# Transposes of fp32 in 64-row tiles, two shared PSUM banks for them and for the rows of x, masks by bank, and constants spread over GpSimd's blocks

## The chip, the cores and the metric

The kernel runs on one core of one Trainium2 chip. The metric is the device time of one execution in microseconds, median of several runs. The engines are named as in the profile: PE is TensorE (PEld its weight loads), DVE VectorE, ACT ScalarE, POOL GpSimd, SP SyncE.

## What is computed

```python
# _attn_ref: q, k, v are [8, 8, 576, 64] (batch, heads, sequence, head_dim)
scores = scale * np.matmul(q, k.transpose(0, 1, 3, 2))
gamma = 1.0 - 2.0 ** (-5.0 - np.arange(H, dtype=np.float32))
Dmat = np.where(rel >= 0, gamma[:, None, None] ** rel[None, :, :], 0.0)
ret = scores * Dmat[None, :, :, :]
attn_out = np.matmul(ret, v)
# reference
x = attn_out.transpose(0, 2, 1, 3).reshape(B * S, H * D)      # [4608, 512]
# _moe_ref: w_gate [512, 8], w1 [8, 512, 1024], w2 [8, 1024, 512]
logits = x @ w_gate
expert_idx = np.argmax(logits, axis=1)
gate_w = probs[np.arange(N), expert_idx]                      # softmax of the logits
for e in range(E):
    mask = expert_idx == e
    out[mask] = gate_w[mask, None] * (np.maximum(x[mask] @ w1[e], 0.0) @ w2[e])
```

## The kernel before

Stage 1 is the attention (a retention with decay), up to about 180 us; stage 2 is the mixture of experts, up to the end. The order of the instructions on each engine is the order in which the program is written (a manual schedule); waits come from the buffers that a tile pool hands out and from the data.

The decay is split into a factor on q and one on k: POOL multiplies them in (`scale_q` L261 writes qq, `scale_k` L271 writes kk). Each batch has 576 positions, in five blocks (b, c): c=0 to 3 have 128 positions, c=4 has the last 64. Within a block the scores are masked, and what earlier blocks contribute comes through a running state (64x64 per head). The loop of L753 goes over the 40 blocks i and issues per block:

- `scale_q` and `scale_k(i+3)` on POOL, and the loads of k and v for block i+6 (q for the batch after the next) on SP; some blocks also load an expert's weights (POOL's queue, L249).
- T: `stage_TK(i+2)` and, for c>0, `stage_TQ` of the next batch. Each makes four fp32 transposes of 128x128 on PE (L63) into one PSUM bank (tiles psk and psq), and ACT copies the bank to SBUF (kT L293, qT L283).
- for c=1 `stage_L2`, the transposed router logits of the batch before.
- R: `stage_R(i-2)`, the bf16 rows of x: four transposes of xb into psr, copied by ACT (xr L420) and stored by SP to x_rows, from which stage 2 gathers.
- S: `stage_S(i+1)` adds k^T v to the state in the bank pss; ACT copies it (se L310). There is none when block i+1 has c=4. The tile se has two buffers, so in blocks c=1 and c=2 its copy waits until IN of the same block has read the older one.
- AV: `stage_AV(i)`, masked scores times v, into the two banks of psx; with c=4 this is part of the next step.
- for c=0 `stage_L1`, the router logits of the batch before, from xT and xTr (psl).
- IN: `stage_IN(i)`, the state times q, added in psx; then ACT copies psx twice, as xT (fp32, L373) and xb (bf16, L376). With c=4 ACT copies one half (xo), DVE adds the other to it (xTr L398), and ACT casts that (xb L401).
- SC: `stage_SC(i+1)`, the scores of the next block, into the two banks of pssc; DVE multiplies all 128x1024 by the mask in one operation (L328).
- from block (4,1) on, steps of the routing for the first half of the tokens, mostly on DVE (`route_first`).

PSUM has eight banks. Before, pssc has two, psx two, pss one, and a pool psw has three, which psk, psq, psr, the logits and the routing, and the first tiles of stage 2 take in turn. The constants of the router (`make_gate`, at i=3) and of the routing (`make_routing`, at i=5) are made on POOL, each in one run ahead of that block's scale_q.

After the loop come `stage_R(38)`, the transposes of the first gathered tokens (pt), `stage_L1(7)` and the first expert's `mm1` with `stage_L2(7)` and `stage_R(39)` between its parts. Stage 2 opens its own PSUM pools after that `mm1`.

## Time and profile before

| what | value |
|---|---|
| median of 3 runs | 350.86 us (349.3 to 351.81) |
| the profiled execution, its own time | 345.89 us |
| its span, first to last instruction | 344.2 us |
| PE busy | 321.0 us (93%) |
| ACT, POOL, DVE busy | 179.8, 200.6, 127.6 us |
| DMA queues | 65.25 MB, mean 190 GB/s |
| mean granted clock of TensorE | 0.985 of full speed |

A busy PE is not a PE at its peak: matmuls are pipelined, and their ends are modelled, so distances between starts say more than durations. In a timeline neighbouring instructions of one kind stand as one row with their count; in brackets is the idle time of the engine before it and what ended that. An fp32 matmul of L60 has two records, an fp32 transpose of L63 one. Blocks (b, c) can be told apart by their PE rows: c=0 has no psq, c=1 has psl from lt, c=3 has no pss, and c=4 has psx from kT.

### The profile page before, as it was taken

The numbers are of one execution on the slowest core, as the hardware profiler recorded it, in microseconds if no ns is written. First come the engines' busy times: TensorE is split into PE (matmuls) and PEld (weight loads), VectorE is DVE, ScalarE is ACT, GpSimd is POOL, SyncE is SP. The second block draws the span as 40 slices with busy tenths as digits, with TensorE's granted clock in tenths as the row PEclk, the third lists the DMA queues.
The fourth block names the chain that finished last, engine by engine and source line by source line (L and its number), as shares of the span: only waits on it lengthen the run. The fifth ranks groups of instructions, "written<-read, shape, count | busy, mean of one in ns | idle before, by whom it ended". The sixth has DMA issues, their size and how long they took to land. (4 is left out here: it accounts for less than half of the span.)

```text
span 344.2 us, 11063 instructions
## 1 busy us (share of the span) xinstructions
PE 321.0 (93%) x4662; PEld 238.2 (69%) x4662; DVE 127.6 (37%) x243; ACT 179.8 (52%) x365; POOL 200.6 (58%) x251
## 2 busy tenths in 40 slices
PE   6897999999999999899969989999999999999991
PEld 5676888888888888688857656555656566565650
DVE  5411422332336786369426852211212121211210
ACT  3554666674766666467555325455453535354440
POOL 3449454635356274884730247787788788887222
PEclk9998999999999999999999989999999999999997
DMA  8999989899987999999799114697999999999211
GB/s 206 236 209 232 232 205 223 204 229 222 212 199 187 239 216 227 230 259 228 146 203 184 60 61 153 125 191 186 201 165 214 213 195 222 214 218 223 83 53 77
DMA packets 112707, 65.25 MB, mean 190 GB/s; under 512 B 83470, under 2 KB 104974, under 8 KB 112656
## 3 DMA queue, kind: packets, MB, share of 16 engines
q0 software_dynamic: 18432, 31.47, 43.8%
q1 hardware_dynamic: 93696, 33.04, 41.4%
q8 instruction: 37, 0.61, 0.8%
q14 instruction: 14, 0.11, 0.1%
q10 hardware_dynamic: 528, 0.02, 0.1%
HBM read 67.13 MB, written 15.20 MB: 239 GB/s over the span
## 5 line engine op out<-in xcount | busy, mean ns | idle before, releaser
L271 POOL TENSOR_TENSOR kk<-kt,kg 128x512 f32<-128x512 f32 x39 | 41.5, 1064 | 69.7 <-PE pss L60 32.1
L715 ACT ACTIVATE ht<-pm 128x384 bf16<-128x384 f32 (+1 forms) x96 | 50.5, 526 | 55.6 <-PE pm L60 54.8
L60 PE MATMUL py<-w2b,ht 128*128 128x512 bf16 x320 | 76.1, 385 | 0.5 <-ACT ht L715 0.5
L60 PE MATMUL pm<-xt,w1b 128*128 128x256 bf16 (+1 forms) x512 | 72.5, 300 | 0.0
L858 DVE TENSOR_SCALAR ys<-py,gat 128x512 f32<-128x512 f32 x40 | 30.0, 750 | 108.6 <-PE py L60 96.8
L859 POOL DMA_INDIRECT out_dram<-ys,tids x40 | 40.9, 1022 | 47.5 <-DVE ys L858 31.0
L60 PEld LDWEIGHTS <-w1b 128*128 128x128 bf16 x512 | 50.0, 98 | 21.9 <-issue 0.6
L328 DVE TENSOR_TENSOR sc<-pssc,mask 128x1024 f32<-128x1024 f32 x32 | 39.1, 1223 | 48.3 <-PE pssc L60 45.9
L60 PEld LDWEIGHTS <-ht 128*128 128x128 bf16 x320 | 30.3, 99 | 31.6 <-issue 2.2
L658 POOL DMA_INDIRECT xg<-x_rows,tidg x40 | 41.0, 1024 | 15.3 <-issue 8.6
L60 PE MATMUL psx<-sc,vt 128*64 128x128 f32 (+1 forms) x640 | 38.6, 268 | 3.0 <-DVE sc L328 1.7
L60 PE MATMUL pssc<-qT,kT 64*64 64x128 f32 (+1 forms) x1024 | 35.0, 251 | 1.6 <-issue 1.5
L700 ACT COPY xt<-pt 128x512 bf16<-128x512 bf16 x40 | 22.7, 587 | 23.7 <-PE pt L63 23.7
L60 PEld LDWEIGHTS psx<-sc,vt 128*64 128x64 f32 (+1 forms) x640 | 30.9, 137 | 5.6 <-ACT kT L293 2.1
L60 PEld LDWEIGHTS pssc<-qT,kT 64*64 64x64 f32 x1024 | 28.7, 133 | 3.3 <-issue 2.7
L293 ACT COPY kT<-psk 128x512 f32<-128x512 f32 x40 | 23.6, 589 | 13.6 <-PE psk L63 13.3
L373 ACT COPY xT<-psx 128x512 f32<-128x512 f32 x32 | 18.9, 590 | 21.8 <-PE psl L60 11.6
L261 POOL TENSOR_TENSOR qq<-qt,qg 128x512 f32<-128x512 f32 x28 | 30.1, 1076 | 0.2
L63 PE MATMUL psk<-ident,kk 128*128 128x128 f32 x160 | 27.0, 293 | 0.8 <-POOL kk L271 0.8
L249 POOL DMA_DIRECT2D w2b<-in_moe_w_dram x32 | 24.0, 781 | 3.8 <-DMA w2b<-in_moe_w_dram 2.7
L310 ACT COPY se<-pss 128x256 f32<-128x256 f32 x32 | 12.4, 389 | 24.4 <-PE psx L60 23.3
L63 PE MATMUL psq<-ident,qq 128*128 128x128 f32 x128 | 19.5, 275 | 4.2 <-POOL qq L261 2.6
(126 smaller groups left out, 368.0 us busy)
## 6 DMA issues: line engine op xcount, KB each, us to landing
kt<-in_k_dram SPq DMA_DIRECT2D x32, 256.0 KB, 5.5
qt<-in_q_dram SPq DMA_DIRECT2D x16, 512.0 KB, 5.1
vt<-in_v_dram SPq DMA_DIRECT2D x32, 256.0 KB, 5.1
w1b<-in_moe_w_dram POOLq DMA_DIRECT2D x32, 256.0 KB, 6.1
w2b<-in_moe_w_dram POOLq DMA_DIRECT2D x32, 256.0 KB, 7.0
x_rows<-xr SPq DMA_DIRECT2D x32, 128.0 KB, 5.1
kt<-in_q_dram SPq DMA_DIRECT2D x8, 128.0 KB, 4.9
kt<-in_k_dram SPq DMA_DIRECT2D x8, 128.0 KB, 4.6
```

Source lines behind the costliest of these rows:

```text
L60: nc.tensor.matmul(out=out, lhsT=lhsT, rhs=rhs, start=start, stop=stop, skip_group_check=True)
L63: nc.tensor.transpose(out=out, in_=in_, identity=identity)
L249: after(nc.gpsimd.dma_start(out=wb[e][part // n][:, o:o + m, :], in_=w[e, o * P:(o + m) * P, :].rearrange("(c p) f -> p c f", p=P)), dep)
L261: eng.tensor_tensor(out=qq[:, :, :].rearrange("p s (h d) -> p h s d", d=DH), in0=qts[b][:, h0:h0 + 2, :, :], in1=qg[:, 0:NCH, h0:h0 + 2].r ...
L271: eng.tensor_tensor(out=kk[:, :, :], in0=kts.pop(i)[:, :, :], in1=kg[:, blocks[i][1], :].unsqueeze(2).to_broadcast([P, H, DH]), op=ALU.mult)
L293: mark["kT"] = nc.scalar.copy(out=kT[:, :, :].rearrange("p a t -> p (a t)"), in_=pst[:, :])
L328: mark["sc"] = nc.vector.tensor_tensor(out=sc[:, :, :, :].rearrange("p j a i -> p (j a) i"), in0=pssc[:, :, :].rearrange("p j (a i) -> p ( ...
L658: nc.gpsimd.indirect_dma_start(out=xg[:, :], out_offset=None, in_=x_rows[0:nr, :], in_offset=bass.IndirectOffsetOnAxis(ap=slots[ph][1][:, ...
L700: nc.scalar.copy(out=xts[(e, ph)][:, :, j * P:(j + 1) * P], in_=pt[:, :, :])
L715: nc.scalar.activation(out=ht[:, f0:f0 + per, :], in_=pm[:, :, :], func=AF.Relu)
L858: nc.vector.tensor_scalar(out=ys[:, :], in0=py[:, :], scalar1=gat[:, i:i + 1], scalar2=None, op0=ALU.mult)
L859: scatters.append(nc.gpsimd.indirect_dma_start(out=next(outs)[:, :], out_offset=bass.IndirectOffsetOnAxis(ap=tids[:, i:i + 1], axis=0), in ...
```

## The change

Five things are done, all in stage 1 and its end.

1. TK and TQ of a block become one `stage_T`. Each transpose of 128 rows becomes two of 64 rows (the upper and the lower half of the array's rows), which write to two different banks. These two banks are one tile pst2 with a single buffer; TK uses the left 256 columns of both banks, TQ the right. Both copies by ACT are issued after all transposes.
2. The rows of x (psr) take the same tag and so the same single buffer as pst2. R's transposes become twice as many, of 64 columns of xb each, and R stands behind AV. The pool psw keeps one bank.
3. The mask is two operations, one for each bank of pssc, and AV goes bank by bank.
4. `make_gate` comes at i=2, between scale_q and scale_k, with the memset of lg; `make_routing` is a generator, of which each block from i=7 on issues one piece.
5. In the first batch two of TQ's four parts go to psx and two to pst2. The PSUM pools of stage 1 are closed, and those of stage 2 opened, before `stage_R(38)`.

On ACT, in a block with c=2 (a full block with a state), this stood before (in brackets the engines and DMA queues whose semaphores an instruction waits for); kT and qT are T's copies, xr is R's, se the state's, xT and xb those of psx:

```order
L293 COPY kT<-psk 128x512 [waits PE_49]
L283 COPY qT<-psq 128x512 [waits PE_49]
L420 COPY xr<-psr 128x512 [waits DMAHW5_49,PE_49]
L310 COPY se<-pss 128x256 [waits PE_49,Activation_49]
L373 COPY xT<-psx 128x512
L376 CAST xb<-psx 128x512
```

and this stands after the change:

```order
L312 COPY kT<-pst_939 128x2x4x64 [waits PE_49]
L298 COPY qT<-pst_939 128x512
L342 COPY se<-pss 128x256 [waits PE_49,Activation_49]
L454 COPY xr<-psr 128x512 [waits DMAHW6_49]
L405 COPY xT<-psx 128x512
L408 CAST xb<-psx 128x512
```

xr has moved behind se, and qT has no wait of its own, since both copies wait for all of T.

On PE, in a block with c=4, this stood before (psk and psq are T, psr is R, pss is S, psx from sc is AV):

```order
L63 MATMUL psk<-ident,kk 128x128 [waits Activation_49,Pool_49]
L63 MATMUL psk<-ident,kk 128x128 x3
L63 MATMUL psq<-ident,qq 128x128 [waits Activation_49,Pool_49]
L63 MATMUL psq<-ident,qq 128x128 x3
L63 LDWEIGHTS xb
L63 MATMUL psr<-identb,xb 128x2x64 [waits Activation_49]
...
L60 MATMUL pss<-vt,kk 64x64 [waits DMAHW2_49]
L60 MATMUL pss<-vt,kk 64x64 x7
L60 MATMUL psx<-sc,vt 64x64 [waits DMAHW7_49,DVE_49,Activation_49]
```

and after the change:

```order
L63 MATMUL pst_660<-ident,kk 128x64 [waits Activation_49,Pool_49]
L63 MATMUL pst_660<-ident,kk 128x64 x7
L63 MATMUL pst_660<-ident,qq 128x64 [waits Pool_49]
L63 MATMUL pst_660<-ident,qq 128x64 x7
L60 MATMUL pss<-vt,kk 64x64 [waits DMAHW2_49]
L60 MATMUL pss<-vt,kk 64x64 x7
L63 LDWEIGHTS xb [waits PE_49]
L63 MATMUL psr<-identb,xb 64x2x64 [waits Activation_49]
...
L60 MATMUL psx<-sc,vt 64x64 [waits DMAHW7_49,DVE_49]
```

R's first transpose waited for nothing but its own input's copy and stood ahead of S; now it stands behind S, and its wait for ACT takes in the copies kT and qT, which read the same buffer.

On POOL, around the constants of the router (wgp), this stood before:

```order
L271 TENSOR_TENSOR kk<-kt,kg 128x512
L261 TENSOR_TENSOR qq<-qt,qg 128x2x4x64
L271 TENSOR_TENSOR kk<-kt,kg 128x512
L226 MEMSET wgp 128x256
L231 COPY wgp<-wgn 64x2x8 x8
L261 TENSOR_TENSOR qq<-qt,qg 128x2x4x64
L271 TENSOR_TENSOR kk<-kt,kg 128x512
```

and after the change:

```order
L269 TENSOR_TENSOR qq<-qt,qg 128x2x4x64
L279 TENSOR_TENSOR kk<-kt,kg 128x512
L269 TENSOR_TENSOR qq<-qt,qg 128x2x4x64
L233 MEMSET wgp 128x256
L238 COPY wgp<-wgn 64x2x8 x8
L244 MEMSET lg 128x320
L279 TENSOR_TENSOR kk<-kt,kg 128x512
L269 TENSOR_TENSOR qq<-qt,qg 128x2x4x64
```

The constants of the router, with lg, have moved ahead of one kk; those of the routing, which stood two pairs of qq and kk later in one run of fourteen with lg's memset, are in pieces of two from the eighth block on.

The diff, cut to its core:

```diff
     wk1 = p1.enter_context(tc.tile_pool(name="wk1", bufs=1))
     attc = p1.enter_context(tc.tile_pool(name="attc", bufs=1))
     rtmp = p1.enter_context(tc.tile_pool(name="rtmp", bufs=1))
-    ps1 = p1.enter_context(tc.tile_pool(name="ps1", bufs=1, space=PSUM))
-    psw = p1.enter_context(tc.tile_pool(name="psw", bufs=3, space=PSUM))
+    pp = ExitStack()
+    ps1 = pp.enter_context(tc.tile_pool(name="ps1", bufs=1, space=PSUM))
+    pst2 = pp.enter_context(tc.tile_pool(name="pst2", bufs=1, space=PSUM))
+    psw = pp.enter_context(tc.tile_pool(name="psw", bufs=1, space=PSUM))
+    pools = {"T": lambda *a: psw.tile(*a, tag="W", name="psw"),
+             "R": lambda *a: pst2.tile(*a, tag="t2", name="psr")}
 
 
...
@@ -272,26 +280,50 @@
                           in1=kg[:, blocks[i][1], :].unsqueeze(2).to_broadcast([P, H, DH]), op=ALU.mult)
         kks[i] = kk
 
-    def stage_TQ(b, p):
+    def pair_banks():
+        return pst2.tile([P, 2, 512], F32, tag="t2", name="pst2")
+
+    def put_TQ(ps, o, b, p):
 
         qq = qqs.pop((b, p))
-        pst = psw.tile([P, 512], F32, tag="W", name="psq")
         for s_ in range(NCH):
-            tr(pst[:, s_:512:NCH], qq[:, s_, :], ident[:, :])
+            for u in range(2):
+                r = slice(u * DH, (u + 1) * DH)
+                tr(ps[:, u, o + s_:o + 256:NCH], qq[r, s_, :], ident[r, r])
+
+    def get_TQ(ps, o, b, p):
+
         if b not in qTs:
             qTs[b] = wkp.tile([P, NP, 512], F32, tag="qT", name="qT")
-        nc.scalar.copy(out=qTs[b][:, p, :], in_=pst[:, :])
-
-    def stage_TK(i):
+        nc.scalar.copy(out=qTs[b][:, p, :].rearrange("p (u t) -> p u t", u=2), in_=ps[:, :, o:o + 256])
+
+    def put_TK(ps, o, i):
+
+        kk = kks[i]
+        for p in range(NP):
+            for u in range(2):
+                r = slice(u * DH, (u + 1) * DH)
+                tr(ps[:, u, o + p * DH:o + (p + 1) * DH],
+                   kk[r, 2 * p:2 * p + 2, :].rearrange("p h d -> p (h d)"), ident[r, r])
+
+    def get_TK(ps, o, i):
+
+        kT = wk3.tile([P, NP, P], F32, tag="kT")
+        mark["kT"] = nc.scalar.copy(out=kT[:, :, :].rearrange("p a (u t) -> p u a t", u=2),
+                                    in_=ps[:, :, o:o + 256].rearrange("p u (a t) -> p u a t", t=DH))
+        kTs[i] = kT
+
+    def stage_T(i, b, p):
+
         if i >= NB:
             return
-        kk = kks[i]
-        pst = psw.tile([P, 512], F32, tag="W", name="psk")
-        for p in range(NP):
-            tr(pst[:, p * P:(p + 1) * P], kk[:, 2 * p:2 * p + 2, :].rearrange("p h d -> p (h d)"), ident[:, :])
-        kT = wk3.tile([P, NP, P], F32, tag="kT")
-        mark["kT"] = nc.scalar.copy(out=kT[:, :, :].rearrange("p a t -> p (a t)"), in_=pst[:, :])
-        kTs[i] = kT
+        ps = pair_banks()
+        put_TK(ps, 0, i)
+        if p is not None:
+            put_TQ(ps, 256, b, p)
+        get_TK(ps, 0, i)
+        if p is not None:
+            get_TQ(ps, 256, b, p)
 
     def stage_S(i):
...
                         r = slice(j * DH, (j + 1) * DH)
                         mm(pssc[u * DH:(u + 1) * DH, j, p * P + u * DH:(p + 1) * P], kT[r, p, u * DH:(u + 1) * DH],
                            qT[r, p, c * P + u * DH:(c + 1) * P], True, True)
-            mark["sc"] = nc.vector.tensor_tensor(
-                out=sc[:, :, :, :].rearrange("p j a i -> p (j a) i"),
-                in0=pssc[:, :, :].rearrange("p j (a i) -> p (j a) i", i=P),
-                in1=mask[:, :].unsqueeze(1).to_broadcast([P, 2 * NP, P]), op=ALU.mult)
+            for j in range(2):
+                mark["sc"] = nc.vector.tensor_tensor(
+                    out=sc[:, j, :, :], in0=pssc[:, j, :].rearrange("p (a i) -> p a i", i=P),
+                    in1=mask[:, :].unsqueeze(1).to_broadcast([P, NP, P]), op=ALU.mult)
         else:
             qTs[(b, "r")] = kT
...
         if c < NCH:
             vt = vts.pop(i)
             sc = scs.pop(i)
-            for p in range(NP):
-                for j in range(2):
+            for j in range(2):
+                for p in range(NP):
                     o = (j ^ (p % 2)) * DH
                     mm(psx[o:o + DH, j, (p // 2) * P:(p // 2 + 1) * P], vt[:, 2 * p + j, :], sc[:, j, p, :],
...
@@ -405,7 +437,7 @@
         b, c = blocks[i]
         full = c < NCH
         n = NP if full else NP // 2
-        ps = psw.tile([P, n * P], BF16, tag="W", name="psr")
+        ps = pools["R"]([P, n * P], BF16)
         xb = xbs.pop(i)
         src = xb[:, :, :].rearrange("p w t -> p (w t)") if full else xb[:, :]
 
@@ -414,7 +446,9 @@
             w, a = k // (n // 2), k % (n // 2)
             o = ps[:, :].rearrange("p (h d) -> p h d", d=DH)
             o = o[:, 4 * a + w:4 * a + w + 3:2, :] if full else o[:, 2 * w:2 * w + 2, :]
-            tr(o, src[:, k * P:(k + 1) * P], (identb, identx)[w][:, :])
+            for u in range(2):
+                r = slice(u * DH, (u + 1) * DH)
+                tr(o[r], src[:, k * P + u * DH:k * P + (u + 1) * DH], (identb, identx)[w][:, :])
         xr = wk4.tile([P, n * P], BF16, tag="xr", name="xr")
         t0 = b * S + c * P
...
@@ -469,24 +502,29 @@
 
     def make_routing():
 
-        nc.gpsimd.memset(lg[:, :, :], 0.0)
         nc.gpsimd.memset(su1[:, :], -1.0)
         nc.gpsimd.affine_select(out=su1[:, :], in_=su1[:, :], pattern=[[-1, P]], base=0, channel_multiplier=1,
                                 compare_op=ALU.is_ge, fill=0.0)
+        yield
         nc.gpsimd.memset(onesb[:, :], 1.0)
         nc.gpsimd.iota(iota_r[:, :], pattern=[[1, P]], base=0, channel_multiplier=0,
                        allow_small_or_imprecise_dtypes=True)
+        yield
         nc.gpsimd.iota(rev[:, :], pattern=[[-1, E]], base=E, channel_multiplier=0,
                        allow_small_or_imprecise_dtypes=True)
         nc.gpsimd.memset(off[:, :], 0.0)
...
@@ -725,17 +763,22 @@
 
     keep_busy(12)
     scale_k(0, nc.vector)
-    stage_TK(0)
-    for p in range(NP):
+    stage_T(0, None, None)
+    for p in range(2):
         scale_q(0, p, nc.vector)
-        stage_TQ(0, p)
-        if p == 1:
-            keep_busy(8)
-            nc.vector.memset(pssc[:, :, :], 0.0)
+        put_TQ(psx, p * 256, 0, p)
+        get_TQ(psx, p * 256, 0, p)
+    keep_busy(8)
+    nc.vector.memset(pssc[:, :, :], 0.0)
+    ps = pair_banks()
+    for p in range(2, NP):
+        scale_q(0, p, nc.vector)
+        put_TQ(ps, (p - 2) * 256, 0, p)
+        get_TQ(ps, (p - 2) * 256, 0, p)
     nc.vector.memset(psx[:, :, 256:512], 0.0)
     scale_k(1)
     scale_k(2)
-    stage_TK(1)
+    stage_T(1, None, None)
     stage_SC(0)
     stage_S(0)
     load_k(5)
...
     for i, (b, c) in enumerate(blocks):
-        if i == 3:
-            make_gate()
-        if i == 5:
-            make_routing()
-
         if c > 0 and b + 1 < B:
             scale_q(b + 1, c - 1)
+        if i == 2:
+            make_gate()
         scale_k(i + 3)
+        if i > 6:
+            next(constants, None)
         fetch(early.get(i, 0))
         load_k(i + 6, mark.get("sc"))
-        stage_TK(i + 2)
-        if c > 0 and b + 1 < B:
-            stage_TQ(b + 1, c - 1)
+        stage_T(i + 2, b + 1, c - 1 if c > 0 and b + 1 < B else None)
         if c == 1 and b > 0:
             stage_L2(b - 1)
-        if i > 1:
-            stage_R(i - 2)
         if c in (1, 3) and b + 2 < B:
             load_q(b + 2, c // 2, mark.get("kT"))
         stage_S(i + 1)
         stage_AV(i)
+        if i > 1:
+            stage_R(i - 2)
         if c == 0 and b > 0:
             stage_L1(b - 1)
...
-    pools = {"T": lambda *a: psw.tile(*a, tag="W", name="pt"), "H": lambda *a: psw.tile(*a, tag="W", name="pm")}
+    pp.close()
+    pq = ExitStack()
+    psT = pq.enter_context(tc.tile_pool(name="psT", bufs=3, space=PSUM))
+    psH = pq.enter_context(tc.tile_pool(name="psH", bufs=3, space=PSUM))
+    psY = pq.enter_context(tc.tile_pool(name="psY", bufs=2, space=PSUM))
+    pools["T"] = pools["R"] = lambda *a: psT.tile(*a, tag="pt", name="pt")
+    pools["H"] = lambda *a: psH.tile(*a, tag="ph", name="pm")
```

## Rows read from the trace of the kernel before

**Rows 1.** Busy us (instructions) of the engines by stretch; granted clock, DMA share, GB/s.

```profile
30.00:33.40 3.40, 3.40 (x48) 2.95 (x45) 0.42 (x1) 1.58 (x4) 3.21 (x11) 0.50 1.19 241
...
40.00:60.00 20.00, 19.77 (x452) 17.36 (x448) 6.38 (x9) 13.10 (x28) 9.13 (x9) 1.00 0.91 218
```

**Rows 2.** Timeline of PE, block (2,2): start us, busy us, operation, count.

```profile
65.59 0.66 PE L63 MATMUL psk<-ident,kk 128*128 128x128 f32 x4
...
66.52 0.28 PE L63 MATMUL psr<-identb,xb 128*128 128x128 bf16 x2
...
66.83 0.69 PE L60 MATMUL pss<-vt,kk 128*64 128x64 f32 x16
67.35 1.05 PE L60 MATMUL psx<-sc,vt 128*64 128x128 f32 x16
68.33 0.67 PE L60 MATMUL psx<-qT,se 64*64 64x128 f32 x16
...
69.80 0.66 PE L63 MATMUL psk<-ident,kk 128*128 128x128 f32 x4
```

**Rows 3.** Timeline of ACT: block (1,4), then the end of block (2,2).

```profile
54.40 0.62 ACT L283 COPY qT<-psq 128x512 f32<-128x512 f32 x1
...
69.11 0.37 ACT L310 COPY se<-pss 128x256 f32<-128x256 f32 x1 [1.27 <-PE psx L60]
69.38 0.59 ACT L373 COPY xT<-psx 128x512 f32<-128x512 f32 x1
69.86 0.60 ACT L376 CAST xb<-psx 128x512 bf16<-128x512 f32 x1
```

**Rows 4.** Timeline of PE, block (1,3).

```profile
49.69 0.66 PE L63 MATMUL psk<-ident,kk 128*128 128x128 f32 x4
...
52.23 0.67 PE L60 MATMUL psx<-qT,se 64*64 64x128 f32 x16
```

**Rows 5.** Timeline of PE, block (1,4).

```profile
53.05 0.66 PE L63 MATMUL psk<-ident,kk 128*128 128x128 f32 x4
...
54.92 0.46 PE L60 MATMUL psx<-sc,vt 64*64 64x64 f32 x16
```

**Rows 6.** Timelines of PE and, last row, of DVE, block (2,0).

```profile
56.41 0.66 PE L63 MATMUL psk<-ident,kk 128*128 128x128 f32 x4
...
57.92 1.09 PE L60 MATMUL psx<-sc,vt 128*64 128x128 f32 x16
58.95 1.08 PE L60 MATMUL psl<-xT,wgp 128*32 128x128 f32 x32
...
56.56 1.22 DVE L328 TENSOR_TENSOR sc<-pssc,mask 128x1024 f32<-128x1024 f32 x1
```

**Rows 7.** Timeline of PE early in stage 1.

```profile
25.87 0.66 PE L63 MATMUL psk<-ident,kk 128*128 128x128 f32 x4
28.74 0.66 PE L63 MATMUL psq<-ident,qq 128*128 128x128 f32 x4 [2.21 <-POOL qq L261]
...
32.55 1.06 PE L63 MATMUL psk<-ident,kk 128*128 128x128 f32 x4
```

**Rows 8.** Timeline of POOL early in stage 1.

```profile
24.66 1.04 POOL L271 TENSOR_TENSOR kk<-kt,kg 128x512 f32<-128x512 f32 x1 [2.61 <-PE psx L60]
...
27.63 1.06 POOL L261 TENSOR_TENSOR qq<-qt,qg 128x512 f32<-128x512 f32 x1
```

**Rows 9.** Groups by line and form, weight loads: busy us, mean ns | idle before.

```profile
L63 PEld LDWEIGHTS psk<-ident,kk 128*128 128x128 f32 x160 | 17.4, 144 | 6.7 <-issue 3.1 <-POOL kk L271 2.3 <-POOL qq L261 0.5
...
L60 PEld LDWEIGHTS psl<-xT,wgp 128*32 128x32 f32 x256 | 6.5, 110 | 2.5 <-ACT xr L420 1.3 <-issue 1.2
```

**Rows 10.** Waits of PE, whole span: total us, times, longest us.

```profile
PE psx L60 <- DVE sc L328: 1.7, 7, 0.4
```

**Rows 11.** Timelines of DVE (first row) and PE at the end of stage 1.

```profile
179.24 0.42 DVE L398 TENSOR_TENSOR xTr<-psx,xo 128x256 f32<-128x256 f32 x1 [1.64 <-ACT xo L396]
...
180.64 1.08 PE L60 MATMUL psl<-xT,wgp 128*32 128x128 f32 x32 [1.10 <-ACT xr L420]
```

21 lines of the change are left out of this document (12 added, 9 removed).

## The prediction

> **What bounds the kernel now.** I read first the busy time by stretch, then TensorE's (PE's) order in time through one batch of stage 1, then what ScalarE (ACT), VectorE (DVE) and GpSimd (POOL) do beside it. In a steady stretch PE is busy 19.77 of 20 us, ACT 13.10, and the DMA engines carry a share of 0.91 [rows 1]: stage 1 goes by PE's order, with ACT and the loads not far behind. The change leaves the expert stage's arithmetic as it is, so every term below lies in stage 1 or at its end. Within a block I count from the start of its transposes (T). A block with c=2 lasts 4.21 us: T 0.93, rows of x (R) 0.31, state S 0.52, AV 0.98, then IN and scores 1.47 up to the next T [rows 2]. Blocks c=3 and c=4 each last 3.36 [rows 4 to 6].
>
> On ACT a copy of 128x512 follows its predecessor after 0.48 us when both are ready (0.27 after the half-sized se), and takes 0.59 to 0.62 [rows 3]. A mask of 1024 columns takes 1.22 us on DVE, and in c=0 AV starts 0.14 after its end (56.56 + 1.22 to 57.92) [rows 6]. I use 0.15 us for one engine's hand-over to another.
>
> **T itself.** TK and TQ are 8 instructions in 0.93 us, 0.116 each [rows 2]; after the change they are 16 that move 64 columns instead of 128. No row shows a 64-row tile with 128 columns. The nearest rows: 16 records of S move 64 columns in 0.52 us where 16 of AV move 128 in 0.98, so halving the columns halves a record; 16 records of IN use 64x64 tiles and take 0.48 for the same 128 columns where AV with 128x64 tiles takes 0.98, so two row halves run side by side [rows 2]. Both together would make T 16 x 0.116 / 4 = 0.47 us. Bounds: 0.47 if it is so, 0.93 if the loading of 128 columns sets the pace and T gains nothing. I take 0.47, because the row nearest in operation (IN's row halves) shows the full effect.
>
> On the load, the trace has 144 ns for one of 128 columns and 128 rows and 110 ns for one of 32 columns [rows 9]: a load overlaps others, and its time hardly follows its columns. The Trainium skill ("TensorE: Matmul & The Clock Gate", section "LDWEIGHTS (loading the stationary operand)") puts a load at columns/1.2 ns, whatever the number of rows: 107 ns for 128 columns, an estimate from that page, by which two 64-row tiles loaded side by side would take as long as one full tile and T would stay as it is. That is rival A's time below; the durations of these two rows do not follow that rule, though they do not settle the pace of a load either.
>
> **What the new order does with it, block by block.** T, TK's and TQ's output and R's output now share one buffer. R waits until both copies have read it, and qT's copy is behind kT's; and R's own copy xr now stands after se and ahead of xT and xb. All other work of a block keeps its length.
>
> c=1: T is 0.46 shorter, nothing new is late (the iteration before copies se without a wait): **-0.45**.
>
> c=2: in the iteration before, se waits for IN, so it starts 0.69 before T (69.11 against 69.80), and xT and xb come after it [rows 3]. With xr between, xb starts at -0.69 + 0.27 + 0.48 + 0.48 = 0.54, ends at 1.14, and AV, which overwrites what xb reads, starts at 1.29. T and S are done at 1.0, so PE waits 0.3. Then AV 0.98, R 0.31, IN and scores 1.47: 4.05 against 4.21, **-0.16**.
>
> c=3: no S. AV starts at 1.29 again; the first mask half, some 0.69 us long (an estimate: half of the 1.22 [rows 6] and 0.08 for a second start), is done before. AV ends at 2.27. kT is copied at 1.02, qT at 1.50 to 2.12, so R may start at 2.27 too. R 0.31, and from AV's end to the next T 0.82 as now (52.23 to 53.05) [rows 4, 5]: 3.40, **+0.04**.
>
> c=4: here R stands behind T and S on PE with no long AV before it. qT is copied 1.35 to 1.97 after T (54.40, 0.62 long) [rows 3, 5], set by xT, xb and kT ahead of it, not by PE; a faster T does not move it. R starts at 2.12, while T and S end at 1.1: 1.0 us of idle PE, and behind R stand AV, IN and the scores of the next block, all of PE's work. R 0.31 and 1.49 from AV to the next T (54.92 to 56.41) [rows 5, 6]: 3.92, **+0.56**.
>
> c=0: only TK. The mask's second half ends at 0.15 + 2 x 0.69 = 1.53, AV's second half (0.49) starts at 1.68, R ends at 2.48, where AV ends 2.54 after T's start now (56.41 to 58.95) [rows 6]: **-0.06**.
>
> Sum: -0.07 us a batch, over seven batches (the first goes by its loads) **-0.5 us**. If nothing waited it would be five TK and four TQ at 0.23 each, 2.1 us a batch: the copies give nearly all of it back.
>
> **The spread constants.** At 28.74 PE waited 2.21 us for a qq of POOL, and then ran at a granted clock of 0.50, the 1.2 GHz level, for 3.4 us [rows 1, 7]. That block lasted 6.68 us (25.87 to 32.55) against 3.36, 3.3 more, and the half clock reached 0.85 us into the next, 0.4 more: 3.7. The cause is on POOL: kk at 24.66, then the gate's memset and copies until qq at 27.63, 1.93 us [rows 8]. The change puts this work ahead of that kk, which waits 2.61 us for PE anyway [rows 8]. With one more memset (lg) it is somewhat over 2 us and fits. qq then runs at 25.70 and is done at 26.76; PE, done with TK at 26.1, waits 0.7 instead of 2.2, and I leave 0.2 for the two copies behind it. 3.7 - 0.9 = **-2.8 us**, between nothing (the wait only moves) and 3.7. The routing constants, in pieces of two, go into POOL's gaps: nothing; a piece that meets a busy POOL costs no more than itself.
>
> **What is dearer.** AV waits for the mask 7 times, 1.7 us, 0.24 each [rows 10]. Once routing shares DVE (from block (4,1)) masks come late, and as AV in c=1 now stands 0.8 us earlier, a late mask is waited for in full: 4 batches by 0.2, an estimate, **+0.8**, from 0 to 1.7 (as much again as now). At the stage's end R of the last full block needs the bank pools closed, so the last xTr read: 179.24 + 0.42 + 0.15 = 179.81. The last logits wait 1.10 us for ACT's xr as it is (180.64) [rows 11], so what comes late there can cost anything from nothing to another 1.1 us; I take the middle, **+0.6**, as R's copy then stands directly in front of that wait. In the start-up, the first q transposes go into other banks at the pace of their loads: nothing, up to one copy (0.6).
>
> Sum: -0.5 - 2.8 + 0.8 + 0.6 = -1.9. The profiled execution took 345.89 us (span 344.2), so 344.0 by its own time; it is 5.0 under the median 350.86 of the runs, and on that median the forecast is **349.0 us**.
>
> **Rivals.**
> A, T is not shortened, the load paces it. Against the forecast c=1 loses 0.45, c=2 0.16, c=3 0.07 and c=4 0.21 (both copies wait for T's end at 0.93 + 0.15, so qT ends at 2.18): 0.9 a batch, 6.3 in all: 355.3, slower. It decides from the point where T takes 0.8 us or more. For it: no row has such a tile, and the 0.116 us of a full tile's step may be its load's as well as its moving columns'. Against it: IN's and S's rows, and loads whose time does not grow with columns. The page's rule above is this rival. Chance 0.20.
> B, the copies keep up and T's gain comes whole: 2.1 instead of 0.07 a batch, 14 us more: 335. For it: ACT is busy only 13.10 of 20 us [rows 1]. Against it: the order of the copies is fixed, and it is their place, not their sum, that binds. 0.05.
> C, the idle 1.0 us of each c=4 draws the 1.2 GHz clock as the 2.21 us did: 3.4 us at 0.50 cost 1.7 [rows 1]. In four of the batches: +6.8, 355.8. Against it: only the longer wait shows it. 0.09.
> D, the early stall is only put off, since the loads, at a share of 1.19 there and 0.91 later [rows 1], cannot come 2.8 us sooner: 351.8. 0.14.
>
> **The numbers.** Forecast 0.52, with a range of its own from 344.5 to 353 (the bounds of the T pattern's hand-overs, some 0.3 us a batch either way, with those of the terms above). 1% either side of 350.86, about what a measurement here can tell, is 347.35 and 354.37. Faster: 0.21 of the forecast, B, 0.02 of D: 0.28. Slower: 0.02 of the forecast, 0.14 of A, C: 0.25. Same: 0.47. The range 343.5 to 357 leaves out B, a part of C, and the far ends.
>
> **What would show it.** In a steady batch: T at 0.47 us; PE idle about 1.0 us before R in c=4, put down to ACT's qT; 0.3 before AV in c=2, put down to xb; T-to-T lengths of 4.62, 4.05, 3.40 and 3.92 for c=0, 2, 3 and 4. Early: qq directly after kk, a wait of 0.7 for it, clock 1.00 from 26 to 36 us. Wrong would be: T at 0.9 (A), no idle before R (B), a clock under 1 in the batches (C), loads waited for by POOL at 28 us and after (D).

## The result and the profile after

The changed kernel is slower: 351.25 us median of 20 runs against 348.44 of 20, ratio 1.012 with a 95% interval of 1.0084 to 1.0157; on another chip 1.0102 (1.0055 to 1.015). The forecast was 349.0 on the first median of 350.86, that is 0.5% faster. The profiled execution took 350.37 us, its span is 348.6 where before had 344.2. Executions of one kernel scatter by 2 to 3%, so every ratio here is taken over those within 1.5% of the fastest of their kernel, and what is under half a per cent is not told apart.

Share and clock, from the page of the changed kernel (sections 1 and 2):

```profile
PE 313.3 (90%) x5094; PEld 232.6 (67%) x5094; DVE 138.1 (40%) x275; ACT 182.1 (52%) x365; POOL 200.7 (58%) x251
...
PEclk9699999999998999998999999999999999999997
```

PE has 8 us less work (321.0 before), and is idle 12 us more. The clock row has low slices near 10, 108 and 160 us; before it had them near 30 and near 200, the second in stage 2.

A steady piece, block (1,4), as PE and then ACT see it (compare [rows 5]):

```profile
50.32 0.46 PE L63 MATMUL pst<-ident,kk 64*128 64x64 f32 x8
...
50.96 0.69 PE L60 MATMUL pss<-vt,kk 128*64 128x64 f32 x16
52.32 0.30 PE L63 MATMUL psr<-identb,xb 128*64 128x128 bf16 x4 [0.68 <-ACT qT L298]
...
54.16 0.46 PE L63 MATMUL pst<-ident,kk 64*128 64x64 f32 x8
...
51.65 0.62 ACT L298 COPY qT<-pst 128x512 f32<-128x512 f32 x1
```

T is done within 0.64 us of its start (50.32 to 50.96, the change of tile shape to S included), where it took 0.93. qT is copied from 51.65 to 52.27, 1.33 to 1.95 after T's start, and R, 52.32, waits for it. The block lasts 3.84 us against 3.36.

The early stall is gone: POOL makes the gate's constants ahead of a kk, and T waits 0.31 and 0.21 us (at 23.23 and 27.09) where it had waited 2.21 ([rows 7, 8]).

```profile
23.49 1.54 POOL L238 COPY wgp<-wgn 64x16 f32<-64x16 f32 x8
...
25.46 1.04 POOL L279 TENSOR_TENSOR kk<-kt,kg 128x512 f32<-128x512 f32 x1
...
27.09 0.46 PE L63 MATMUL pst<-ident,kk 64*128 64x64 f32 x8 [0.21 <-issue]
```

Where the time came from is seen best where each block's kT is copied on ACT (from the timelines; block n's copy stands two blocks ahead of its use; us):

| kernel | block 2 | 6 | 21 | 26 | 34 | 37 | 39 | 21 to 39 |
|---|---|---|---|---|---|---|---|---|
| before | 13.65 | 33.70 | 94.61 | 114.71 | 150.34 | 161.55 | 170.36 | 75.75 |
| changed | 16.35 | 31.25 | 90.69 | 113.94 | 151.29 | 166.91 | 175.44 | 84.75 |
| changed, other chip | 14.81 | 30.72 | 92.19 | 114.78 | 152.83 | 167.62 | 176.14 | 83.95 |

Up to block 21 the change is 2.4 to 3.9 us ahead. From there, where the routing of the first tokens shares the engines, it loses 8 to 9 us: some 2 between blocks 23 and 26, 4 between 34 and 37. This is measured against the one profile of the kernel before, and not all of it belongs to the change: three probes below leave that kernel's late blocks as they are, and there 21 to 39 takes 77.88 to 79.01. From block 39's copy to the end it is 173.8 us before and 173.2 after on this chip, and 176 to 180 in every profile from another chip, so stage 1 alone is compared here.

What PE waited for from 95 to 182 us, first before, then after (total us, times, longest):

```profile
PE psx L60 <- DVE sc L328: 1.1, 4, 0.4
```

```profile
PE psx L60 <- DVE sc L361: 6.0, 3, 3.6
PE psr L63 <- ACT qT L298: 3.8, 4, 1.9
```

Together that is 8.7 us more than before, 5.5 of it in two single waits.

The first late stall, in block (4,2): DVE, ACT and PE, and the clock after it.

```profile
104.56 1.08 DVE L538 TENSOR_TENSOR d<-lg,mx 128x160 f32<-128x160 f32 x1
...
105.68 0.34 ACT L542 ACTIVATE ex<-d 128x160 f32<-128x160 f32 x1 [1.88 <-DVE d L538]
...
106.39 0.59 ACT L298 COPY qT<-pst 128x512 f32<-128x512 f32 x1
...
107.03 0.30 PE L63 MATMUL psr<-identb,xb 128*64 128x128 bf16 x4 [1.90 <-ACT qT L298]
...
107.80:111.50 3.70, 3.70 (x70) 3.25 (x60) 1.86 (x3) 2.67 (x6) 1.20 (x2) 0.54 1.15 253
```

DVE's d (1.08 us, 0.39 before) is late, the exponential ex on ACT waits 1.88 us for it, kT and qT stand behind ex, and R waits 1.90 us for qT. The granted clock of the next 3.7 us is 0.54, that is mostly the level of 1.2 GHz. Before, ex waited 1.38 us in the same place, and PE waited for nothing, as R had another bank than kT and qT.

The second, in block (6,3): DVE, POOL, PE and the clock.

```profile
150.70 5.33 DVE L614 TENSOR_SCALAR pos<-pos 128x20 f32<-128x20 f32 x1
...
158.13 1.28 DVE L361 TENSOR_TENSOR sc<-pssc,mask 128x512 f32<-128x512 f32 x2
...
150.69 1.05 POOL L279 TENSOR_TENSOR kk<-kt,kg 128x512 f32<-128x512 f32 x1
151.67 0.61 POOL L257 DMA_DIRECT2D w1b<-in_moe_w_dram  x1
152.29 1.08 POOL L269 TENSOR_TENSOR qq<-qt,qg 128x512 f32<-128x512 f32 x1
153.32 1.05 POOL L279 TENSOR_TENSOR kk<-kt,kg 128x512 f32<-128x512 f32 x1
154.31 0.60 POOL L257 DMA_DIRECT2D w1b<-in_moe_w_dram  x1
154.92 1.07 POOL L269 TENSOR_TENSOR qq<-qt,qg 128x512 f32<-128x512 f32 x1
155.94 1.05 POOL L279 TENSOR_TENSOR kk<-kt,kg 128x512 f32<-128x512 f32 x1
...
158.96 1.70 PE L60 MATMUL psx<-sc,vt 128*64 128x128 f32 x16 [3.61 <-DVE sc L361]
...
159.00:162.50 3.50, 3.50 (x56) 3.17 (x56) 2.47 (x5) 0.87 (x2) 0.00 (x0) 0.54 0.69 142
```

A DVE operation on 20 elements a partition, which begins with POOL's kk at 150.69, lasts 5.33 us, while POOL goes from kk to a weight load to qq without a gap; the mask comes after it at 158.13, and AV waits 3.61 us. Again the clock falls to 0.54. Before, the same operation (L576) took 0.27 us. It ends at 156.03, just after POOL's qq (155.99), though POOL goes on with the next kk at once.

There is a third wait of this kind, which no run takes away by itself:

```profile
133.21 1.16 PE L60 MATMUL psx<-sc,vt 128*64 128x128 f32 x16 [1.50 <-DVE sc L361]
```

The mask stands there behind three routing products (rh) that take DVE 4.15 us beside POOL's qq and kk, where three took 3.51 before.

### The profile page after: what moved, and what is told of

Read it like the earlier page. It is cut to its first block, busy times and chain, and to the rows that moved or that the text cites. A ratio compares the mean times of both kernels' runs of the same rounds, so it can differ in the third digit from the quotient of the medians.

```text
span 348.6 us, 11915 instructions
## 1 busy us (share of the span) xinstructions
PE 313.3 (90%) x5094; PEld 232.6 (67%) x5094; DVE 138.1 (40%) x275; ACT 182.1 (52%) x365; POOL 200.7 (58%) x251
## 5 line engine op out<-in xcount | busy, mean ns | idle before, releaser
L60 PE MATMUL py<-w2b,ht 128*128 128x512 bf16 x320 | 74.5, 379 | 0.0
L361 DVE TENSOR_TENSOR sc<-pssc,mask 128x512 f32<-128x512 f32 x64 | 41.2, 685 | 45.8 <-PE pssc L60 41.1
L60 PE MATMUL psx<-sc,vt 128*64 128x128 f32 (+1 forms) x640 | 40.0, 273 | 7.8 <-DVE sc L361 6.0
L60 PE MATMUL pssc<-qT,kT 64*64 64x64 f32 (+1 forms) x1024 | 36.2, 258 | 0.4 <-issue 0.4
L60 PEld LDWEIGHTS pssc<-qT,kT 64*64 64x64 f32 x1024 | 29.9, 137 | 1.7 <-issue 1.0
L312 ACT COPY kT<-pst 128x512 f32<-128x512 f32 x40 | 23.9, 597 | 12.6 <-PE pst L63 12.2
L454 ACT COPY xr<-psr 128x512 bf16<-128x512 bf16 (+1 forms) x38 | 20.9, 549 | 18.3 <-PE psr L63 17.4
L60 PE MATMUL pss<-vt,kk 128*64 128x64 f32 x512 | 22.6, 231 | 1.1 <-issue 1.0
```

The lines of the kernel that those rows point to most:

```text
L60: nc.tensor.matmul(out=out, lhsT=lhsT, rhs=rhs, start=start, stop=stop, skip_group_check=True)
L312: mark["kT"] = nc.scalar.copy(out=kT[:, :, :].rearrange("p a (u t) -> p u a t", u=2), in_=ps[:, :, o:o + 256].rearrange("p u (a t) -> p u ...
L361: mark["sc"] = nc.vector.tensor_tensor(out=sc[:, j, :, :], in0=pssc[:, j, :].rearrange("p (a i) -> p a i", i=P), in1=mask[:, :].unsqueeze( ...
L454: nc.scalar.copy(out=xr[:, :], in_=ps[:, :])
```

## The experiments

Theory: R's wait for the copies lets ex reach PE, and POOL's unbroken work holds DVE; each is followed by a half clock. Rivals: the loads pace the late blocks anyway, so that what is freed is waited for elsewhere; or a part of the change costs by itself. All ratios are to the kernel before on the same chip.

### Parts alone and undone

**The constants alone**, in the kernel before (the diff's part 4).

> The kernel before with the constants of GpSimd spread as in the change, and nothing else of it. Theory (the early stall goes, and it is worth what the changed kernel was ahead at its sixth block): 2 us less than before, about 346.5 where before has 348.4. Rival (loads only put the stall off): no difference beyond 0.5 us, though the wait for qq at 28.74 us is gone.

Measured: 0.9968 (0.993 to 1.0007). Block 6 comes 2.9 us earlier (30.77), block 39 no earlier (170.66): between 21 and 39 it needs 78.38 us. DVE and PE of this kernel:

```profile
149.38 2.31 DVE L583 TENSOR_SCALAR pos<-pos 128x20 f32<-128x20 f32 x1
...
156.06 1.09 PE L60 MATMUL psx<-sc,vt 128*64 128x128 f32 x16 [2.43 <-DVE sc L331]
```

The early gain is there, and 2.0 us of it go between blocks 34 and 37 (13.22 us, 11.21 before), where the held operation stands. So such a loss does not need the new order on PE. The time agrees with the rival: no difference clear of noise.

**The change without the constants.**

> The changed kernel with the constants in two runs as before. Theory (parts add up): about 2 us above the changed kernel, 353 us, so 1.3% above before. Rival (the constants have nothing to do with the late losses, but POOL's place in time decides whether DVE is held up): the 5.33 us DVE operation at 150.7 us may be gone, and then it is 2 us below the changed kernel, 349.

Measured: 1.0072 (1.003 to 1.0114), if anything under the changed kernel. Both expectations missed: the time does not rise to 1.3% above before, and the held operation is not gone (3.37 us). Block 6 is at 32.09, without the early stall, though the constants stand where they did; its start is slower (block 2 at 17.91), which gives POOL the time. The parts do not add up: at block 6 the constants are worth 2.9 us in the kernel before and about 1 in the changed one.

**Full tiles** in the changed order (TQ likewise):

```diff
-            for u in range(2):
-                r = slice(u * DH, (u + 1) * DH)
-                tr(ps[:, u, o + p * DH:o + (p + 1) * DH], kk[r, 2 * p:2 * p + 2, :]..., ident[r, r])
+            tr(ps[:, o // 256, p * P:(p + 1) * P], kk[:, 2 * p:2 * p + 2, :]..., ident[:, :])
```

> The changed kernel with transposes of 128 rows again, TK in one of the two banks and TQ in the other; order, buffers, waits and all else as changed. Theory (the tiles do what they should, T 0.93 against 0.47, and the order takes most of it back): 0.9 us a batch more than the changed kernel, its batch at 20.7 us, 6 us in all: ratio to before 1.03. Rival (the 64-row tiles bring nothing, since the copies decide): same as the changed kernel, 1.012.

Measured: 1.0107 (1.004 to 1.0174). PE in block (1,4):

```profile
54.39 0.65 PE L63 MATMUL pst<-ident,kk 128*128 128x128 f32 x4
...
55.41 0.69 PE L60 MATMUL pss<-vt,kk 128*64 128x64 f32 x16
56.69 0.30 PE L63 MATMUL psr<-identb,xb 128*64 128x128 bf16 x4 [0.60 <-ACT qT L296]
...
58.53 0.66 PE L63 MATMUL pst<-ident,kk 128*128 128x128 f32 x4
```

T takes 1.02 to S, the block 4.14, a batch 20.82 (blocks 12 to 17), where the profiles with 64-row tiles in this order have 19.63 to 19.99: 0.8 to 1.2 more, as the theory said. Block 21 comes at 97.22, 5 to 6.5 us behind the changed kernel; yet the whole time is the same, since from 21 to 39 it takes 81.53: its held operation lasts 0.75 us, and the two late waits of PE are 0.82 and 1.59 us instead of 1.90 and 3.61. Here the rival was right about the total and wrong about the reason.

**One mask operation** and AV in its former order.

```diff
-            for j in range(2):
-                mark["sc"] = nc.vector.tensor_tensor(out=sc[:, j, :, :], in0=pssc[:, j, :]...
+            mark["sc"] = nc.vector.tensor_tensor(out=sc[:, :, :, :]..., in0=pssc[:, :, :]...
...
-            for j in range(2):
-                for p in range(NP):
+            for p in range(NP):
+                for j in range(2):
```

> The changed kernel with one mask operation of 1024 columns for both banks, and AV in its order of before. Theory (the halves let AV start in c=0 and c=3, but cost DVE 0.08 us per block more): c=0 and c=3 are longer, 0.2 to 0.5 us a batch together, 2 to 3 us in all before the late stalls; ratio 1.015 to 1.02. Rival (c=0 and c=3 are bound by ACT's copies, and the split brings nothing): 1.011 as with the changed kernel.

Measured: 1.0256 (1.0192 to 1.0319), 5 us more than the changed kernel. AV in c=0:

```profile
58.33 1.09 PE L60 MATMUL psx<-sc,vt 128*64 128x128 f32 x16 [0.44 <-DVE sc L360]
```

AV waits for the mask in two blocks of five, 0.44 us in c=0 and 0.52 in c=3, and a batch takes 20.99 us (blocks 12 to 17), a whole microsecond more. Of the late stalls the second stays (3.07 us for the mask, the operation held 3.55); R's wait for qT in block (4,2) is 0.73 us. So the shorter T is of use only with the split mask.

### The two stalls

**The changed kernel again**, on another chip, to see whether the two stalls belong to it or to one execution.

> The changed kernel itself, beside the others on one chip. Theory: 1.012 again, with stalls of 6.5 us at block 24's kT and of 8 us at block 36's in its profile, so that they belong to the program and not to one execution. Rival (chance of one execution): one or both stalls are missing.

Measured: 1.0102 (1.0055 to 1.015). Block 24's kT comes 6.90 us after block 23's, block 36's 7.13 after 35's, and the held operation lasts 3.43 us: the stalls belong to it. The half clock after the first does not:

```profile
108.73 0.30 PE L63 MATMUL psr<-identb,xb 128*64 128x128 bf16 x4 [2.02 <-ACT qT L298]
...
108.50:112.00 3.50, 2.84 (x76) 2.39 (x77) 2.06 (x4) 2.31 (x6) 1.24 (x2) 1.00 1.07 201
```

PE waits a little longer than on the first chip, and the clock after it is 1.00. After the second stall (2.84 us) it falls (0.66 from 160 to 164 us).

**The exponential later**, first with a DVE step moved along, then with DVE's order as it was (the second diff):

```diff
         ex = pool.tile([P, GT, E], F32, tag="ex")
-        nc.scalar.activation(out=ex[:, :, :], in_=d[:, :, :], func=AF.Exp)
         yield 0.2
...
+        nc.scalar.activation(out=ex[:, :, :], in_=d[:, :, :], func=AF.Exp)
         nc.vector.tensor_tensor(out=oh[:, g, :, :].rearrange("p e t -> p t e"), in0=t[:, :, :],
```

> The changed kernel with the routing's exponential issued to ACT five DVE operations later, so that ACT doesn't stand waiting for DVE's d in front of kT and qT. Theory (R waits for qT, which waits behind the exponential): the block of 6.58 us at 102.9 us becomes 4.1, the granted clock there stays at 1.00, and the time falls by 2.4 us to about 349. Rival (the loads or POOL bind later anyway): the block shortens, and a later one lengthens by as much: 351.

Measured: 1.010 (1.0049 to 1.0151). The wait of PE at 107 us went, and the step that moved into block (4,1) put DVE's oh (1.74 us, beside a kk of POOL) ahead of the next mask:

```profile
111.23 1.16 PE L60 MATMUL psx<-sc,vt 128*64 128x128 f32 x16 [2.15 <-DVE sc L361]
```

> The changed kernel with the exponential issued to ACT together with the next block's first routing step, DVE's order and the steps of each block as they were. The first try moved a DVE step too, and got a new wait for the mask. Theory (R waits for qT, which waits behind the exponential, and a half clock follows; about 2.4 us and nothing else is touched): block 24's kT comes 4.1 us after block 23's instead of 6.5, and the ratio to before is 1.004 against 1.011 for the changed kernel. Rival (what is won there is waited for later, at the held DVE operation): 1.01 again, with the stall at block 36 longer than 8 us.

Measured: 0.9988 (0.9941 to 1.0034), some 1.1% under the changed kernel. Block 24's kT comes 4.41 us after block 23's (6.51 and 6.90 in the changed kernel; 6.10 in the kernel before, where the exponential delays the copy but nothing on PE), and ACT goes from xb to kT to qT without a wait:

```profile
106.24 0.62 ACT L408 CAST xb<-psx 128x512 bf16<-128x512 f32 x1
106.72 0.62 ACT L312 COPY kT<-pst 128x512 f32<-128x512 f32 x1
107.21 0.63 ACT L298 COPY qT<-pst 128x512 f32<-128x512 f32 x1
```

The held operation lasts 1.85 us here, and AV of block (6,3) waits 2.23 us for its mask; block 36's kT comes 5.21 us after block 35's (8.00 and 7.13 in the changed kernel), so this rival does not hold.

**No routing steps while POOL works without a gap:**

```diff
-        if rf is not None:
+        if rf is not None and i not in (31, 32):
             steps(rf, 1.6)
```

> The changed kernel with no routing steps issued in the blocks (6,1) and (6,2); they follow one after the other from (6,3) on. Theory (a small DVE operation that starts while POOL works through qq, kk and weight loads without a gap is held until the gap, 5.33 us, and the mask behind it with it): the wait of 3.61 us for the mask and the half clock after it go, 4 us less, 347. Rival (the mask is late because POOL's kk and qq or the loads are): the wait stays, or stands one block later, and the time is 351. If the held operation only meets another run of POOL, it shows in a later block.

Measured: 1.0053 (1.0022 to 1.0084). The held operation and AV of block (6,3):

```profile
161.57 0.17 DVE L614 TENSOR_SCALAR pos<-pos 128x20 f32<-128x20 f32 x1
...
158.94 1.09 PE L60 MATMUL psx<-sc,vt 128*64 128x128 f32 x16 [0.22 <-ACT xb L408]
```

0.17 us, with POOL idle, and AV's wait is down from 3.61 to 0.22. The gain, about 0.6% and with an interval that touches the changed kernel's, is half of what I expected: blocks 34 to 37 are 3.3 us shorter, but 23 to 26 are 0.9 longer and 30 to 32 1.4 (0.3 on the other chip). The edit moves all routing operations of two blocks, so it does not single out the held one. In the late blocks of the first two probes below, which are the kernel before's, that operation takes 0.81 and 0.90 us, and AV waits 1.94 and 1.78 us all the same, as two products after it (ohb) take 2.55 and 2.52 instead of 1.50.

**Both** (the second form of the exponential), twice:

> The changed kernel with both late stalls taken away: the exponential is issued to ACT with the next block's first routing step (DVE's order unchanged), and no routing steps in blocks (6,1) and (6,2). Theory (these two stalls with their half clocks make the loss): no block over 5.5 us, 6 us less than the changed kernel, ratio to before 0.995. Rival (as the exponential alone showed, a stall taken away in the routing blocks comes back as another, since DVE, POOL and loads are behind there): ratio 1.005 or more, with a new wait for the mask or for POOL.

> The changed kernel without its two late stalls, as e8_exp_hold, whose profile showed a disturbed execution. Theory: ratio 0.9925 again within its interval, and in the profile no wait over 1.7 us of PE between 95 and 170 us, block 24's kT after 4.1 us and block 36's after 5 us or less. Rival (the first ratio came from how few undisturbed runs it had): 1.000 or more.

Measured: 0.9925 (0.9875 to 0.9975), then 0.9993 (0.9948 to 1.0037). So the loss goes, by 1.1 to 1.9%, and what is left is no difference, or a little faster. The medians of all executions say the same in smaller steps: the changed kernel lies 0.8 and 1.4% above before, without the first stall 0.6%, without the second 0.5%, without both 0.1% above and 0.4% below. In the second profile blocks 24 and 36 follow at 4.14 and 3.20 us, block 39's kT is at 169.69 (175.44 changed, 170.36 before). But 21 to 39 still takes 78.97, and block 30's kT comes 7.58 us after block 29's, with a wait of 1.74 us for a mask behind other DVE operations (125.37 us) and a half clock behind it; 2.08 us at 174.56 are put down to "issue". The rival holds for this remainder, which is no more than the kernel before shows in the probes.

**The constants and the hold** in the kernel before:

> The kernel before with the spread constants (0.997 as measured) and no routing steps in blocks (6,1) and (6,2). With the constants alone the mask was waited for 2.43 us at 156 us, behind a DVE operation of 2.31 us. Theory (this wait and its half clock gave back the early gain): ratio 0.99. Rival (the late blocks are paced by something else): 0.997 again.

Measured: 0.9928 (0.9885 to 0.9971). Block 39 at 169.56; 21 to 39 takes 76.22. This is the one edit of the kernel before whose interval lies under 1. The hold alone was not run in that kernel, so how the gain is shared between the two parts is not shown.

### R in a bank of its own

```diff
-             "R": lambda *a: pst2.tile(*a, tag="t2", name="psr")}
+             "R": lambda *a: psw.tile(*a, tag="W", name="psr")}
...
+        if i > 1 and c != 1:
+            stage_R(i - 2)
         stage_S(i + 1)
         stage_AV(i)
-        if i > 1:
+        if i > 1 and c == 1:
             stage_R(i - 2)
```

> The changed kernel, but the rows of x (R) in the one bank of psw instead of the transposes' two, and in front of S again except in blocks with c=1 (there behind AV). So R waits for neither kT's nor qT's copy, and xr is copied ahead of se again. Theory (that wait alone gives back the shorter transposes): no idle second in c=4, batches of 18.1 us instead of 20.1 before and 19.8 changed, six of them by 2 us each, and the stall of 1.90 us for qT behind the exponential at 107 us gone: ratio to before about 0.97. Rival (the loads, at a DMA share of 0.91 to 1.0, set the pace): batches stay above 19 us, POOL waits for kt more, and the ratio is 0.99 or more. The held DVE operation at 150 us may be there in either case (3.6 us and a half clock).

> The changed kernel with both late stalls taken away (the exponential issued with the next block's first routing step, no routing steps in blocks (6,1) and (6,2)) and R in psw's bank, in front of S except in c=1. Theory (the stalls cost about 2%, R's wait for the copies about another 1%): ratio to before 0.98 or less. Rival (both fixes free the same time, since loads or POOL pace the late blocks): 0.99, like the one with the stalls taken away alone (0.9925).

Measured: 0.9978 (0.9937 to 1.0018), and with both stalls taken away 0.9982 (0.9946 to 1.0018). PE of the first in block (1,4), and in block (5,1):

```profile
50.70 0.46 PE L63 MATMUL pst<-ident,kk 64*128 64x64 f32 x8
...
53.65 0.46 PE L63 MATMUL pst<-ident,kk 64*128 64x64 f32 x8
...
126.03 0.25 PE L63 MATMUL psr<-identb,xb 128*64 128x128 bf16 x2 [1.90 <-DVE lg L484]
```

c=4 is 2.95 us long (3.84), without a wait for qT: the price that I put on that wait was nearly right. But both ratios missed, and the batches (blocks 12 to 17: 19.94 and 19.79) did not come to 18.1: "issue" waits up to 1.2 us lie between, and in the routing blocks R, now in the bank of the logits and ranks, waits up to 1.90 us for DVE's reads of them, in the second run too. So the rival's figure holds; that the loads are its reason is not shown. In the second, block 21's kT is at 88.59, the earliest of all, and stage 1's last at 167.57, in an execution of 345.25 us; other executions took up to 354.85. I could not tell what makes these differ.

### The held operation by itself

Three probes in the kernel before: eight extra products on POOL in a run in three blocks, and one small DVE operation behind the mask there and in three blocks without the run. The first writes all products to one buffer, the others to four in turn.

```diff
+        for n in range(8 if i in (10, 12, 14) else 0):
+            nc.gpsimd.tensor_tensor(out=busy_o[n % 4][:, :], in0=busy_a[:, :], in1=busy_a[:, :], op=ALU.mult)
...
+        small(probe.get(i))
```

> The kernel before with small extra operations, that write to scratch tiles alone: in blocks (2,0), (2,2) and (2,4) POOL gets eight extra products of 128x512 in one run, and DVE one small operation behind the mask (in turn a tensor_scalar of 128x20, a reduction of 128x160 to 128x20, and a scalar_tensor_tensor of 128x20 with two inputs); in blocks (3,1), (3,2) and (3,3) DVE gets the same three without the run. Theory (POOL working without a gap holds DVE operations that use a second read of SBUF): 0.17 to 0.3 us each without the run, and with it a tensor_scalar and a scalar_tensor_tensor that last as long as what is left of the run, 2 us and more; the reduction, with one input, not. Rival (the 5.33 us were a wait for something else): 0.17 to 0.3 us in all blocks.

> The probe of the held operation again, but the eight products of POOL write to four tiles in turn, so that one starts before the last has ended, as qq and kk do; in the first probe each waited for the one before, and the small operations ended with the product that was running (0.41 and 0.80 us instead of 0.17). Theory (DVE gets in only where POOL leaves a gap): now a tensor_scalar or scalar_tensor_tensor that meets the run lasts until its end, 2 us or more. Rival (it is held for one POOL operation at most, and the 5.33 us had another reason): 1.1 us at most, as in the first probe.

> The probe with four tiles for POOL's products once more, with the operations placed otherwise: the tensor_scalar in blocks (2,2) and (2,4), where the scalar_tensor_tensor was held 7.11 us in the last probe, and the scalar_tensor_tensor in (2,0); without POOL's run a tensor_scalar in (3,1) and (3,2), a scalar_tensor_tensor in (3,3). Theory (both kinds are held until POOL leaves a gap, and the 0.81 us of the tensor_scalar was a product's end that happened to let it in): the tensor_scalar in (2,4) lasts some 7 us. Rival (only the one with two SBUF inputs is held for more than one product): the tensor_scalar lasts 1.1 us at most in both places, and the scalar_tensor_tensor in (2,0) 2 us or more.

Measured, DVE and POOL of the first (each product waits for the one before), the second and the third (products overlap), and each operation without the run:

```profile
89.48 0.80 DVE L765 SCALAR_TENSOR_TENSOR tino<-tiny 128x20 f32<-128x20 f32 x1
...
82.50 8.87 POOL L780 TENSOR_TENSOR busy_o<-busy_a 128x512 f32<-128x512 f32 x8
```

```profile
84.22 7.11 DVE L765 SCALAR_TENSOR_TENSOR tino<-tiny 128x20 f32<-128x20 f32 x1
...
103.33 0.17 DVE L765 SCALAR_TENSOR_TENSOR tino<-tiny 128x20 f32<-128x20 f32 x1
...
79.81 8.01 POOL L780 TENSOR_TENSOR busy_o<-busy_a 128x512 f32<-128x512 f32 x8
```

```profile
77.26 14.81 DVE L761 TENSOR_SCALAR tino<-tiny 128x20 f32<-128x20 f32 x1
...
96.55 0.17 DVE L761 TENSOR_SCALAR tino<-tiny 128x20 f32<-128x20 f32 x1
...
82.01 8.02 POOL L780 TENSOR_TENSOR busy_o<-busy_a 128x512 f32<-128x512 f32 x8
...
90.99 1.05 POOL L261 TENSOR_TENSOR qq<-qt,qg 128x512 f32<-128x512 f32 x1
97.95 1.04 POOL L271 TENSOR_TENSOR kk<-kt,kg 128x512 f32<-128x512 f32 x1 [5.91 <-PE pss L60]
```

A scalar_tensor_tensor of 20 elements takes 0.17 us alone, 0.80 beside products with a gap of 0.08 us between them, 7.11 beside a run without one. A tensor_scalar takes 0.17 alone, and 14.81 from 77.26, while POOL goes through a weight load, four operations, the eight products and two more, to the end of its qq at 92.04. So it is not only the kind with two SBUF inputs that is held. But the runs without a gap also let both kinds in at the end of the product that was running (0.81 and 0.82 us in block (2,0)), so that the gap is what matters is not shown; and the tensor_scalar in (2,4), of which I expected 7 us, began after the run and took 0.17. The reduction, with one input, took 0.31 everywhere.

The theory that DVE gets in only where POOL leaves a gap does not fit. In these profiles 19 small operations (the probes' and the routing's pos) lasted 0.7 us or more. Each ended within 0.07 us of the end of a POOL operation, be it a product or, for the 7.11, a weight load's issue (91.39), in 15 of them with POOL's next one already under way, and only at 92.04 did POOL then pause for more than 0.1 us. So a held operation gets in at the end of a POOL operation, but not always of the first; what picks the one is open.

The Trainium skill ("GPSIMD Engine Reference", section "1. Specifications") says that GpSimd's SBUF interfaces are shared with VectorE, with contention for instructions in a 2-port mode or with two SBUF inputs. The probes agree for the scalar_tensor_tensor, which has two; whether the tensor_scalar runs in such a mode no run shows. What they show of the cost is not a slower operation, but one that waits, at times for many POOL operations.

## Why the prediction was wrong

**The step that failed** is the term "what is dearer", +0.8 us with 0 to 1.7 as its bounds. The stretch that it priced, from block 21 on, took 8 to 9 us more; up to there the two profiles of the changed kernel were ahead by 3.9 and 2.4, both more than the whole forecast gain of 1.9. I saw that masks come late once DVE shares its time, and priced that by the waits of the kernel before (0.24 each), as if the same lateness would be paid once more. Instead masks cost 6.0 us in three waits from 95 us on, where they had cost 1.1. Two things were not in that price. The first was in the program's order: I wrote that R waits for qT, and that what stands ahead of qT on ACT sets it, and listed xT, xb and kT, but not the routing's exponential, which waits for DVE in one block. Taking it away gave 1.1%. The second no row of before showed at its size (0.27 us for the operation that took 5.33): DVE operations held by POOL, of which the exponential's input d (1.08 us, 0.39 before) and the third wait (1.50 us) seem to be cases too. Keeping the routing out of two blocks gave about 0.6%. A half clock followed both stalls in the first profile (0.54 for 3.7 and 3.5 us), and only the second on the other chip; I had charged one to the early stall and to rival C alone.

**T**: right in kind, a little short. 0.47 us forecast, 0.57 in c=2 and 0.64 in c=4 with the change of tile shape, 0.93 before; full tiles cost 0.8 to 1.2 us a batch, about what rival A was priced at (0.9). So rival A fell: 16 loads of 128 columns lie within 0.64 us. By the rule in the Trainium skill ("TensorE: Matmul & The Clock Gate", section "LDWEIGHTS (loading the stationary operand)") a load of 128 columns takes 128/1.2 ns = 107 ns, so that 16 loads, two row halves side by side, would take an estimated 8 x 107 ns, 0.86 us. The measurement is below that.

**The batch**: sign and place right, size a little short. -0.07 us forecast, -0.3 measured (blocks (2,0) to (3,0): 19.77 against 20.11). By blocks, c=0 to 4: foreseen 4.62, 4.05, 4.05, 3.40, 3.92; measured 4.44, 4.29, 4.11, 3.09, 3.84 (4.68, 4.50, 4.21, 3.36, 3.36 before). In c=4 R comes 2.00 after T (2.12 foreseen), and the wait before it is 0.68, not 1.0, because S ends 1.32 after T, not 1.1. c=1 saved half of its forecast, as T is 0.64 there. The waits for xb were misplaced: ahead of c=2 xr is a half-sized copy, which I had priced as a whole one, and AV waits for nothing; in c=3 AV starts 0.93 after T, not 1.29 (67.00 to 67.93), with a wait of 0.22. So the sum is better than its terms.

**The early stall**: the cause and its cure were right (POOL's gate work runs ahead of kk, T waits 0.2 to 0.3). Blocks 2 to 6 take 14.90 us, where before they took 20.05: 5.1 less, more than the 2.8 forecast. The price of the half clock in it was one execution's: in the three probes, whose early blocks are the kernel before's, T waits 1.35, 2.15 and 2.34 us there, the half clock follows only the last, and blocks 2 to 6 take 17.77, 18.14 and 20.70. And the start-up gave 1.2 to 2.7 back, which I had at nothing, up to 0.6: block 2's kT comes at 13.7 to 14.6 in the profiles with the old start-up and at 13.9 to 18.7 with the new. With one buffer for T, its transposes wait for ACT's copies there, and in the first profile PE runs partly at half clock (1.00 in both of these stretches before):

```profile
8.00:12.00 4.00, 2.69 (x32) 1.97 (x28) 2.08 (x4) 1.67 (x3) 1.04 (x1) 0.64 1.05 196
12.00:16.00 4.00, 3.77 (x60) 3.24 (x62) 1.04 (x2) 0.76 (x3) 1.04 (x1) 0.51 1.04 249
```

**The end**: +0.6 forecast, +0.4 (block 39's kT to the first expert's matmul, 11.8 against 11.4).

**The rivals**: B fell (the copies do bind in c=4). C did not happen where I put it: the waits of 0.68 us in c=4 drew no lower clock, at 40 to 60 us it is 1.00; it happened after late stalls. D, as I put it, fell: the early gain is there until block 21. But a remainder of 3 us between blocks 21 and 39, against the one profile of before, was taken away by no fix of the changed kernel; what paces it stays open, as do the waits put down to "issue".

## What to carry to other kernels

When two stages come to share a buffer, list everything that can stand ahead of the copies that free it, in every block, the rare ones too: a wait that was harmless on ACT becomes a wait of PE. A gain early in a pipeline is only as good as the slack of the late part that has to keep up with it, so price that part by its own engines, not by the waits it has now. Take a stall, and the clock after it, from more than one execution before you price it. And keep small DVE operations with two SBUF inputs or in tensor_scalar form away from unbroken runs of GpSimd.
